# Shifted v rows of the first chunk by matmuls instead of a DRAM bounce, and the first 512 tokens in four passes of 128

## The chip, the cores and the metric

The kernel runs on one core of a Trainium2 chip. The metric is the device time of one execution in microseconds (us); lower is better. The kernel before has a median of 639.02 us over six runs (636.22 to 643.5). The profile that is read here is one execution of 640.18 us.

## The reference

A block of a transformer with 2048 tokens of width 576. A vector c gives six modulation vectors. The first half is attention with 32 heads of 18 elements in which each token looks at itself and at the tokens 2, 4, ... 14 places earlier (window W = 8, dilation 2). The second half is a gated product of width 4608 without an activation.

```python
mod = (silu(c) @ w_mod).reshape(1, 6, 1, 576)       # sa, ca, ga, sb, cb, gb
h = layernorm(x) * (1 + ca) + sa
q, k, v = split(h @ wqkv)                            # 32 heads of 18
idx = pos[:, None] - arange(8)[None, :] * 2          # masked where below 0
logits = einsum('bhsd,bhswd->bhsw', q, k[idx]) * 18 ** -0.5
o = einsum('bhsw,bhswd->bhsd', softmax(logits), v[idx])
x = x + ga * (o @ wo)
h = layernorm(x) * (1 + cb) + sb
x = x + gb * (((h @ w_gate) * (h @ w_up)) @ w_down)
```

## The kernel before

**Tiling.** The tokens are cut into chunks (`SIZES`: 128, 128, then seven of 256). The gate/up and down products work on 512 tokens (`CM`), which `DOWN` groups: the first 512 tokens take three passes over the gate and up weights (128, 128 and 256 tokens), each later 512 take one pass. After the last pass of a group follows the down product (`down`, L534). Weights of gate and up come in nine blocks of 512 columns. A ring of three buffers (`gm`, `gr`) streams them; the four blocks named in `KEPT` lie in the space of `wd`, the weights of down, until the first group's last pass is done with them. Then `block_done` loads that space with w_down, quarter by quarter (L271). `ORDER` is the order of the blocks in each pass.

**Attention of one chunk** has two generators. `project` does layernorm (L308 to L318), turns the rows into columns (`turn`, L325), applies sa and ca (L335, L337), and makes q, k (L360, evacuated by ACT at L362), the last 64 rows of both (L366 to L371) and v (L377). v is cast by ACT into `v_sb` with its elements in the order (d, h) (L380) and written to DRAM, `vd`, by ACT's DMA queue (L383). `attend` reads vd back through POOL's queue (L397): four shifted copies of each v row per load, two loads for 128 tokens, into `vsh` (three buffers). DVE multiplies q by shifted k (L410), PE sums over d (L419), PE transposes the logits (L427), DVE and ACT do the softmax (L437 to L445). Then DVE weights the v rows by attn (L450) and adds them in a tree (L451, L454, L455). The last addition writes `o_sb` in the order (h, d), one element in every 18th place. PE turns o_sb and multiplies by wo (L465); DVE applies ga, adds x and does the second layernorm; `h2T` is what gate and up read.

**Order of the work.** In the start, up to the first gate/up matmul, PE, DVE and ACT run in the order of the program (`manual_schedule`): `go` draws a generator forward to a named point. `warm` and the matmuls on zeros in `mod_columns` (L203) are filler for PE. `mod_columns` and `mod_row` (L219) make the modulation vectors. In the passes, `Pacer` hands out the pieces of the next chunks' attention between the matmuls of gate/up and down by the fractions in `AT`. Up to `AUTO` passes the engines' order is the scheduler's; after that PE's is the program's. Each engine executes in its own order, waits included. SP's queue loads the weights, ACT's queue writes vd, POOL's reads it and stores the output.

**PSUM.** `att` tiles have two buffers and serve all of attention; `ps_mlp` tiles have three and serve gate/up, down, mod_row and mod_columns.

## Time and profile before

| | |
|---|---|
| profiled execution | 640.18 us, its span 638.5 us |
| PE, DVE, ACT, POOL busy | 588.9, 343.8, 257.5, 49.2 us |
| first gate/up matmul | 54.1 us |
| first 512 tokens finished by PE | 252.2 us |
| vsh loads (L397) | 32 of 576 KB, median 5.4 us from issue to landing |
| vd writes (L383) | 16 of 144 KB, median 1.8 us |
| o_sb addition (L455) | 16, mean 2626 ns |
| vsh multiplication (L450) | 32, mean 1354 ns |

PE is the matmul, PEld its weight load, DVE, ACT and POOL the vector, scalar and general engines, SP the queue that issues most transfers; a small q after an engine marks what its queue issues. A row of the timeline has start, duration, engine, line, operation, and in brackets the idle time before it with what ended it. A row of a stretch has its bounds and length, then busy time of PE, PEld, DVE, ACT and POOL with the number of instructions, the granted TensorE clock as a share of full speed, the busy share of the DMA engines and their GB/s.

### The profile page before, as it was taken

To read this page: it belongs to the slowest core of one execution; us is meant where nothing else is said; L and a number is where in the kernel's file an instruction comes from. 1 tells how busy PE (TensorE), PEld (TensorE's weight loads), DVE (VectorE), ACT (ScalarE), POOL (GpSimd) and SP (SyncE) were. 2 spreads that over 40 slices of the span, in tenths; PEclk is the share of its full clock that TensorE was granted. 3 is DMA by queue.
4 is the path that set the end of the run, shared out by engine and by line. 5 is a ranking of instruction groups with operands and counts; after the bars stand their busy time and mean duration, and the time that the engine had idled before them with its cause. 6 is when DMAs were issued, how large, how long until landed. Compare 5 with 4: busy or idle time off the path is not lost.

```text
span 638.5 us, 11463 instructions
## 1 busy us (share of the span) xinstructions
PE 588.9 (92%) x4802; PEld 377.3 (59%) x4837; DVE 343.8 (54%) x654; ACT 257.5 (40%) x430; POOL 49.2 (8%) x97
## 2 busy tenths in 40 slices
PE   8759989779499989998999999989999999999996
PEld 4437868558377877454435786444446873333675
DVE  2455858857735786594548753683538732121111
ACT  2515565355336224444655223544552024444300
POOL 2101001100010111000000100001000000000000
PEclk9976989889889999999999999998999999999999
DMA  9999465407550042254510230434501003442000
GB/s 262 274 327 289 158 224 159 159 2 223 186 200 5 20 135 74 91 178 149 175 38 18 68 103 20 144 116 168 179 9 38 20 10 112 139 139 65 1 20 20
DMA packets 61133, 75.23 MB, mean 118 GB/s; under 512 B 4618, under 2 KB 54554, under 8 KB 61082
## 3 DMA queue, kind: packets, MB, share of 16 engines
q1 hardware_dynamic: 52970, 49.87, 25.9%
q0 software_dynamic: 5664, 22.12, 9.8%
q10 hardware_dynamic: 2448, 2.51, 1.1%
q8 instruction: 38, 0.62, 0.4%
q14 instruction: 13, 0.11, 0.0%
HBM read 69.75 MB, written 4.74 MB: 117 GB/s over the span
## 4 chain that ended last, share of the span: by engine, by line
PE 53%; DVE 11%; issue 8%; DMA 4%; ACT 1%; POOL 0%; SPq 0%; POOLq 0%; DVEq 0%; ACTq 0%
PE pgu L484 26%; PE acc L534 16%; PE pgu L491 4%; DMA vsh<-vd 3%; DVE vsh L450 3%; PE pv L377 2%; PE pw L465 2%; DVE vsh L451 1%; PE lgT L419 1%; DVE o_sb L455 1%; PE turnA L325 1%; ACT gu L521 1%; DVE hh L522 1%; PE pq L360 1%; DMA gr<-in_B_w_up_dram 1%
## 5 line engine op out<-in xcount | busy, mean ns | idle before, releaser
L484 PE MATMUL pgu<-h2T,gm 128*128 128x512 bf16 (+2 forms) x1313 | 241.9, 334 | 3.1 <-ACT gu L521 1.0
L521 ACT CAST gu<-pgu 128x1024 bf16<-128x1024 f32 (+1 forms) x162 | 140.6, 919 | 144.1 <-PE pgu L491 135.5
L484 PEld LDWEIGHTS <-gm 128*128 128x128 bf16 x1344 | 118.0, 100 | 109.4 <-issue 19.6
L534 PE MATMUL acc<-wd,hh 128*128 128x288 bf16 x1152 | 146.9, 286 | 0.0
L522 DVE TENSOR_TENSOR hh<-gu 128x512 bf16<-128x512 bf16 (+1 forms) x162 | 64.2, 401 | 133.7 <-ACT gu L521 133.7
L534 PEld LDWEIGHTS <-hh 128*128 128x128 bf16 x1152 | 111.9, 98 | 29.1 <-issue 1.7
L410 DVE TENSOR_TENSOR prod<-qT,kT 128x1280 bf16<-128x1280 bf16 (+1 forms) x72 | 46.3, 689 | 22.0 <-PE lgT L419 21.9
L450 DVE TENSOR_TENSOR vsh<-vsh,attn 128x2304 bf16<-128x2304 bf16 x32 | 42.5, 1354 | 14.5 <-DMA vsh<-vd 14.4
L397 POOL DMA_DIRECT2D vsh<-vd x32 | 24.2, 757 | 274.2 <-DMA vd<-v_sb 128.2
L360 PE MATMUL pq<-hT,wqk 128*128 128x256 bf16 (+1 forms) x360 | 42.9, 273 | 2.2 <-ACT hT L337 1.5
L377 PE MATMUL pv<-wv,hT 128*128 128x288 bf16 x160 | 25.0, 296 | 19.4 <-DVE kT L371 18.0
L455 DVE TENSOR_TENSOR o_sb<-vsh 128x576 bf16<-128x576 bf16 x16 | 42.0, 2626 | 0.3
L539 DVE TENSOR_TENSOR y<-acc,gb_bc 128x576 bf16<-128x576 f32 x16 | 12.3, 769 | 54.2 <-PE acc L534 54.2
L491 PE MATMUL pgu<-h2T,gr 64*128 64x512 bf16 (+2 forms) x336 | 40.1, 330 | 1.2 <-DMA gr<-in_B_w_up_dram 0.3
L360 PEld LDWEIGHTS <-wqk 128*128 128x128 bf16 x360 | 33.4, 105 | 10.5 <-issue 4.5
L484 PE MATMUL pgu<-h2T,wd 128*128 128x128 bf16 (+1 forms) x384 | 34.7, 244 | 0.2 <-DVE h2T L335 0.2
L377 PEld LDWEIGHTS <-hT 128*128 128x128 bf16 x160 | 15.1, 100 | 27.3 <-issue 22.3
L484 PEld LDWEIGHTS <-wd 128*128 128x128 bf16 x384 | 29.0, 101 | 3.8 <-issue 1.0
L317 ACT ACTIVATE xn<-x_t,ln_nmr,ln_rstd 128x576 bf16<-128x576 bf16 x32 | 27.6, 862 | 8.1 <-issue 4.2
L380 ACT CAST v_sb<-pv 128x288 bf16<-128x288 f32 x32 | 11.6, 405 | 39.0 <-PE pv L377 35.4
L308 DVE BATCH_NORM_STATS2 ln_stats<-x_t 128x6 f32<-128x288 bf16 x64 | 25.8, 440 | 0.4
L465 PE MATMUL pw<-wo,oT 128*128 128x288 bf16 x160 | 24.9, 306 | 1.0 <-DVE oT L458 0.9
(102 smaller groups left out, 397.4 us busy)
## 6 DMA issues: line engine op xcount, KB each, us to landing
vsh<-vd POOLq DMA_DIRECT2D x32, 576.0 KB, 5.4
gm<-in_B_w_gate_dram SPq DMA_DIRECT2D x27, 512.0 KB, 3.6
gm<-in_B_w_up_dram SPq DMA_DIRECT2D x27, 512.0 KB, 4.8
wd<-in_B_w_down_dram SPq DMA_DIRECT2D x4, 1152.0 KB, 5.8
wm<-in_w_mod_dram SPq DMA_DIRECT2D x4, 576.0 KB, 7.0
vd<-v_sb ACTq DMA_DIRECT2D x16, 144.0 KB, 1.8
out_dram<-y POOLq DMA_DIRECT2D x16, 144.0 KB, 2.0
wd<-in_B_w_gate_dram SPq DMA_DIRECT2D x4, 512.0 KB, 4.4
```

What stands on the lines that cost most here:

```text
L317: nc.scalar.activation(xn[:, j, 0:D], src[j][:], ACTF.Identity, bias=nmr[:, j:j + 1], scale=rstd[:, j:j + 1])
L360: nc.tensor.matmul(pq[:, gi, 0:C], lhsT=wqk[:, kt, w0:w0 + P], rhs=hT[:, kt, 0:C], start=(kt == 0), stop=(kt == KT - 1))
L377: nc.tensor.matmul(pv[q][:], lhsT=hT[:, kt, j * P:(j + 1) * P], rhs=wv[:, kt, q * 288:(q + 1) * 288], start=(kt == 0), stop=(kt == KT - 1))
L410: nc.vector.tensor_tensor(prod[:, 0:nm, 0:C], qT[:, 0:nm, 0:C], kT[:, 0:nm, off:off + C], ALU.mult)
L450: nc.vector.tensor_tensor(vsh[:], vsh[:], attn[:, j, ws, None, :].to_broadcast([P, WG, DH, H]), ALU.mult)
L455: nc.vector.tensor_tensor(o_sb[:, j, 0:D].rearrange("p (h d) -> p d h", d=DH), va[:, 0], va[:, 1], ALU.add)
L465: nc.tensor.matmul(pw[q][:], lhsT=oT[:, m, j * P:(j + 1) * P], rhs=wo[:, m, q * 288:(q + 1) * 288], start=(m == 0), stop=(m == KT - 1))
L484: nc.tensor.matmul(out(t), lhsT=gm[:, kt, t, i * P:(i + 1) * P], rhs=h2[:, kt, cs], start=(kt == 0 and (t == 0 or C > 256)), stop=False, s ...
L491: nc.tensor.matmul(outs[hf](t), lhsT=gr[rows, t, i * P:(i + 1) * P], rhs=h2[rows, KT - 1, cs], start=False, stop=True, skip_group_check=True)
L521: nc.scalar.copy(g, src)
L522: nc.vector.tensor_tensor(hh[:, fs, cs], g[:, :, 0, :], g[:, :, 1, :], ALU.mult)
L534: nc.tensor.matmul(acc[:, q, 0:288], lhsT=hh[:, f, j * P:(j + 1) * P], rhs=wd[:, f, q * 288:(q + 1) * 288], start=(f == 0), stop=(f == FT ...
```

## The change

For the first chunk of 128 tokens v is no longer read back from DRAM. A wider identity (`identw`) whose column window is moved by 2(7-w) is the stationary operand of two matmuls for each of the eight shifts; ACT copies each result into a `vsh` buffer. v is still written to vd, since chunk 1 reads it. DVE multiplies two shifts at a time by attn, and instead of DVE's additions 40 matmuls against the identity (five for each shift) add up in PSUM, which yields o in columns (`oTa`, `oTb`) without `turn`.

The order of o is (d, h) everywhere now: the last addition on DVE writes o_sb in place order, and wo is loaded with its rows in that order, by four transfers on ACT's queue, issued in the start after the first layernorm.

The first 512 tokens are four chunks and four passes of 128; `ORDER`, `AUTO`, `DOWN`, the pass in which the kept blocks are given up and the loads of x follow. There are 29 block loads into the ring instead of 27.

In the start, chunk 1's projection is drawn after the attention of chunk 0 is through, `mod_columns` for the second layernorm has no filler and stands before chunk 0's product with wo, and two warm matmuls are gone. DVE instead of ACT casts chunk 0's k. The short xn activations come after the long ones.

```diff
--- before.py
+++ after.py
@@ -31,17 +31,20 @@
 CH = 256
-SIZES = [128, 128, 256, 256, 256, 256, 256, 256, 256]
-DOWN = [[[0], [1], [2]], [[3, 4]], [[5, 6]], [[7, 8]]]
+SIZES = [128, 128, 128, 128, 256, 256, 256, 256, 256, 256]
+DOWN = [[[0], [1], [2], [3]], [[4, 5]], [[6, 7]], [[8, 9]]]
 FB = 4
-AUTO = 3
+AUTO = 4
 GU_BUFS = 3
 NB = FT // FB
-ORDER = [[0, 1, 2, 3, 4, 5, 6, 7, 8], [6, 7, 8, 5, 4, 3, 2, 1, 0], [2, 3, 4, 5, 8, 1, 0, 6, 7],
-         [0, 6, 7, 1, 2, 3, 4, 5, 8], [4, 5, 8, 0, 1, 2, 3, 6, 7], [3, 6, 7, 0, 1, 2, 4, 5, 8]]
+ORDER = [[0, 1, 2, 3, 4, 5, 6, 7, 8], [6, 7, 8, 5, 4, 3, 2, 1, 0], [8, 1, 0, 5, 4, 3, 2, 6, 7],
+         [2, 3, 4, 5, 0, 6, 7, 1, 8], [7, 1, 8, 0, 2, 3, 4, 5, 6], [4, 5, 6, 0, 1, 2, 3, 7, 8],
+         [3, 7, 8, 0, 1, 2, 4, 5, 6]]
 KEPT = [2, 3, 4, 5]
+KEPT_PASSES = 4
+LOAD_X = {3: 6, 4: 7, 6: 8, 7: 9}
 AT = dict(lg0=.06, lg1=.14, lgT=.19, hT=.24, q0=.29, q1=.34, k0=.39, k1=.44, qkr=.48, v0=.52, v1=.57,
-          oT=.66, wo0=.70, wo1=.74, h2T=.92)
+          ws=.64, oT=.66, wo0=.70, wo1=.74, h2T=.92)
@@ -90,10 +93,11 @@
-    ident = consts.tile([P, P], BF, name="ident")
-    nc.gpsimd.memset(ident[:], 0.0)
-    nc.gpsimd.affine_select(out=ident[:], in_=ident[:], compare_op=ALU.not_equal, fill=1.0, base=0,
-                            pattern=[[-1, P]], channel_multiplier=1)
+    identw = consts.tile([P, HALO + P], BF, name="identw")
+    nc.gpsimd.memset(identw[:], 0.0)
+    nc.gpsimd.affine_select(out=identw[:], in_=identw[:], compare_op=ALU.not_equal, fill=1.0, base=HALO,
+                            pattern=[[-1, HALO + P]], channel_multiplier=1)
+    ident = identw[:, HALO:HALO + P]
     ind = consts.tile([P, KT + 1, H], BF, name="ind")
@@ -176,7 +180,6 @@
     load_rows(nc.sync, wmC[:, :, D:2 * D], w_mod[:, 5 * D:6 * D])
-    load_rows(nc.sync, wo, A_wo)
     wmB = wm_tile()
@@ -184,9 +187,14 @@
+    def load_wo():
+        for dl in range(4):
+            n = len(range(dl, DH, 4))
+            nc.scalar.dma_start(wo[dl * H:(dl + 1) * H, 0:n, :], A_wo.rearrange("(h d) n -> h d n", d=DH)[:, dl::4, :])
+
     def silu_c():
         pc = att([P, KT], BF, "pc")
-        nc.tensor.transpose(pc[:], c_row[:], ident[0:KT, 0:KT])
+        nc.tensor.transpose(pc[:], c_row[:], identw[0:KT, HALO:HALO + KT])
         c_f = sp.tile([P, KT], F32, name="c_f")
@@ -196,11 +204,12 @@
-    def mod_columns(wm, vi):
-        pw = ps_mlp.tile([P, 2, 512], F32, name="warm", tag="mlp")
+    def mod_columns(wm, vi, fill):
+        pw = ps_mlp.tile([P, 2, 512], F32, name="warm", tag="mlp") if fill else None
         pm = ps_mlp.tile([P, 2, 512], F32, name="pm", tag="mlp")
         for kt in range(KT):
-            nc.tensor.matmul(pw[:, 0, :], lhsT=zeros[:, 0:P], rhs=zeros[:, 0:512], start=True, stop=True)
+            if fill:
+                nc.tensor.matmul(pw[:, 0, :], lhsT=zeros[:, 0:P], rhs=zeros[:, 0:512], start=True, stop=True)
             for bi in range(2):
@@ -249,7 +258,7 @@
         for b in order:
-            if b in KEPT and pi < 3:
+            if b in KEPT and pi < KEPT_PASSES:
                 continue
@@ -271,7 +280,7 @@
     def block_done(pi, b):
-        if pi == 2 and b in KEPT:
+        if pi == KEPT_PASSES - 1 and b in KEPT:
             k = KEPT.index(b)
@@ -315,6 +324,7 @@
             nc.scalar.activation(xn[:, j, 0:D], src[j][:], ACTF.Identity, bias=nmr[:, j:j + 1], scale=rstd[:, j:j + 1])
+        for j in range(ST):
             nc.scalar.activation(xn[:, j, D:], src[j][:, D - 64:], ACTF.Identity, bias=nmr[:, j:j + 1], scale=rstd[:, j:j + 1])
@@ -337,6 +347,8 @@
     scale = float(DH) ** -0.5
+
+    v_first = []
@@ -359,7 +371,8 @@
                                      start=(kt == 0), stop=(kt == KT - 1))
-            nc.scalar.copy(qT[:, m0:m0 + 2, 0:C] if t == 0 else kT[:, m0:m0 + 2, HALO:HALO + C], pq[:, :, 0:C])
+            (nc.vector.tensor_copy if ci == 0 and t == 1 else nc.scalar.copy)(
+                qT[:, m0:m0 + 2, 0:C] if t == 0 else kT[:, m0:m0 + 2, HALO:HALO + C], pq[:, :, 0:C])
         yield "qkr"
@@ -381,13 +394,23 @@
             nc.scalar.dma_start(vd[r0:r0 + P, :], v_sb[:])
+        if ci == 0:
+            v_first.extend(vshp.tile([P, WG, DH, H], BF, name="vsh") for _ in range(2))
+            for w in range(W - 1, -1, -1):
+                yield f"s{w}"
+                ps = ps_mlp.tile([P, 2, 512], F32, name="pvs", tag="mlp")
+                off = HALO - DIL * (W - 1 - w)
+                for q in range(2):
+                    nc.tensor.matmul(ps[:, q, 0:288], lhsT=identw[:, off:off + P], rhs=v_sb[:, q * 288:(q + 1) * 288],
+                                     start=True, stop=True)
+                nc.scalar.copy(v_first[w // WG][:, w % WG].rearrange("p (q d) h -> p q (d h)", q=2), ps[:, :, 0:288])
...
         x_t = x_tiles[ci]
-        if ci >= 2:
-            load_x(ci + 4, nc.gpsimd)
+        if ci in LOAD_X:
+            load_x(LOAD_X[ci], nc.gpsimd)
         vshs = {}
@@ -397,8 +420,9 @@
-        for u in ((0, 0), (0, 1), (1, 0))[0:ST + 1]:
-            load_vsh(*u)
+        if ci > 0:
+            for u in ((0, 0), (0, 1), (1, 0))[0:ST + 1]:
+                load_vsh(*u)
         lgs = small.tile([P, 2, CH], BF, name="lgs", bufs=1)
@@ -410,7 +434,7 @@
                 if i % 2 == 1:
-                    if i % WG == 1:
+                    if i % WG == 1 or ci == 0:
                         yield f"lg{g}"
@@ -443,18 +467,34 @@
         nc.vector.tensor_tensor(attn, dd, ssum[:, :, None, :].to_broadcast([P, ST, W, H]), ALU.mult)
-        for j in range(ST):
-            va, vb = vshs[j, 0], vshs[j, 1]
-            for hf, vsh in ((0, va), (1, vb)):
-                ws = slice(hf * WG, (hf + 1) * WG)
-                nc.vector.tensor_tensor(vsh[:], vsh[:], attn[:, j, ws, None, :].to_broadcast([P, WG, DH, H]), ALU.mult)
-            nc.vector.tensor_tensor(va[:], va[:], vb[:], ALU.add)
-            if j + 1 < ST:
-                load_vsh(j + 1, 1)
-            nc.vector.tensor_tensor(va[:, 0:2], va[:, 0:2], va[:, 2:4], ALU.add)
-            nc.vector.tensor_tensor(o_sb[:, j, 0:D].rearrange("p (h d) -> p d h", d=DH), va[:, 0], va[:, 1], ALU.add)
-        yield "oT"
-        banks = turn(o_sb, C)
+        if ci == 0:
+            banks = (att([P, 3, P], F32, "oTa"), att([P, 2, P], F32, "oTb"))
+            for w0 in range(W - 2, -1, -2):
+                vsh = v_first[w0 // WG]
+                ws = slice(w0 % WG, w0 % WG + 2)
+                nc.vector.tensor_tensor(vsh[:, ws], vsh[:, ws], attn[:, 0, w0:w0 + 2, None, :].to_broadcast([P, 2, DH, H]), ALU.mult)
+                yield "ws"
+                flat = vsh[:].rearrange("p w d h -> p (w d h)")
+                for w in (w0, w0 + 1):
+                    for m in range(KT):
+                        f0 = w % WG * D + m * P
+                        n = min(P, WG * D - f0)
+                        nc.tensor.matmul(banks[m // 3][0:n, m % 3, :], lhsT=flat[:, f0:f0 + n], rhs=ident,
+                                         start=(w == W - 2 and m in (0, 3)), stop=(w == 1), skip_group_check=True)
+            yield "oT"
+        else:
+            for j in range(ST):
+                va, vb = vshs[j, 0], vshs[j, 1]
+                for hf, vsh in ((0, va), (1, vb)):
+                    ws = slice(hf * WG, (hf + 1) * WG)
+                    nc.vector.tensor_tensor(vsh[:], vsh[:], attn[:, j, ws, None, :].to_broadcast([P, WG, DH, H]), ALU.mult)
+                nc.vector.tensor_tensor(va[:], va[:], vb[:], ALU.add)
+                if j + 1 < ST:
+                    load_vsh(j + 1, 1)
+                nc.vector.tensor_tensor(va[:, 0:2], va[:, 0:2], va[:, 2:4], ALU.add)
+                nc.vector.tensor_tensor(o_sb[:, j, 0:D].rearrange("p (d h) -> p d h", d=DH), va[:, 0], va[:, 1], ALU.add)
+            yield "oT"
+            banks = turn(o_sb, C)
         (nc.vector.tensor_copy if ci == 0 else nc.scalar.copy)(oT[:, 0:3, 0:C], banks[0][:, :, 0:C])
@@ -592,20 +632,33 @@
         warm(5)
         a0 = project(0)
         next(a0)
-        mod_columns(wmA, 0)
+        load_wo()
+        mod_columns(wmA, 0, True)
         go(a0, "q0")
         warm(3)
+        go(a0, "v0")
+        b0, a1 = attend_into_place(0), project(1)
+        next(b0)
+        go(a0, "s7")
+        next(b0)
+        next(a0)
+        next(b0)
+        next(a0)
+        next(b0)
+        next(a0)
+        go(a1, "hT")
+        next(b0)
+        next(a0)
+        go(b0, "ws")
         go(a0, None)
-        b0, a1 = attend_into_place(0), project(1)
-        go(b0, "lgT")
-        go(a1, "hT")
-        go(b0, "oT")
         mod_row(wmC, 0, ga_bc)
         mod_row(wmC, 1, gb_bc)
+        go(b0, "oT")
+        go(a1, "q0")
+        go(b0, "wo0")
+        mod_columns(wmB, 2, False)
+        go(b0, "h2T")
         go(a1, None)
-        warm(2)
-        go(b0, "h2T")
-        mod_columns(wmB, 2)
         setup_late()
         go(b0, None)
```

## The prediction

> **What bounds the kernel now.** First the page: PE is busy 92% of the span, and the missing tenths lie almost all before slice 16 (255 us). So the question is what PE waits for there. Second, the busy time by stage: the stretches are the start (to 54.1, the first gate/up matmul), the three passes over the first 512 tokens, and the down projection of those tokens.
> ```profile
> span 638.5 us, 11463 instructions
> ...
> PE   8759989779499989998999999989999999999996
> ...
> PEclk9976989889889999999999999998999999999999
> ```
> ```profile
> 54.10:88.10 34.00, 31.55 (x457) 26.74 (x457) 23.99 (x59) 20.06 (x44) 4.07 (x8) 0.95 0.74 238
> 88.10:136.90 48.80, 40.73 (x560) 33.84 (x561) 36.40 (x76) 24.93 (x54) 4.26 (x7) 0.92 0.36 118
> 136.90:201.30 64.40, 55.25 (x520) 43.16 (x520) 38.34 (x69) 29.58 (x47) 4.75 (x7) 0.90 0.48 153
> 201.30:252.20 50.90, 49.19 (x450) 39.24 (x448) 37.18 (x64) 15.60 (x33) 7.47 (x13) 1.00 0.21 71
> ```
> Columns: stretch, length, busy PE, PEld, DVE, ACT, POOL, granted clock, DMA share, GB/s. From 54.1 to 252.2 PE idles 198.1 - 176.7 = 21.4 us; the granted clock (0.95, 0.92, 0.90) takes up to 0.05 x 34 + 0.08 x 48.8 + 0.10 x 64.4 = 12 more, part of them while PE idles anyway. Third, PE in order of time: where the bounce of v through DRAM ends last.
> ```profile
> 36.95 0.38 PE L227 MATMUL warm<-zeros 128*128 128x512 bf16 x1
> 43.39 0.50 PE L325 MATMUL turnA<-ident,o_sb 128*128 128x128 bf16 x3 [6.06 <-DVE o_sb L455]
> 43.69 0.42 PE L325 MATMUL turnB<-ident,o_sb 128*128 128x128 bf16 x2
> 45.04 2.58 PE L465 MATMUL pw<-wo,oT 128*128 128x288 bf16 x10 [0.94 <-DVE oT L458]
> ```
> The bounce leaves 6 us visible; the rest of it (v written at 21.8, vsh in at 34.1 and 37.1) covers chunk 1's projection (29.8 to 36.9). Fourth, DVE around the worst stall, 8.39 us before pv at 175.06:
> ```profile
> 160.77 2.63 DVE L455 TENSOR_TENSOR o_sb<-vsh 128x576 bf16<-128x576 bf16 x1
> ...
> 167.82 1.36 DVE L450 TENSOR_TENSOR vsh<-vsh,attn 128x2304 bf16<-128x2304 bf16 x1 [3.84 <-DMA vsh<-vd]
> 169.21 1.36 DVE L451 TENSOR_TENSOR vsh<-vsh 128x2304 bf16<-128x2304 bf16 x1
> 170.60 0.76 DVE L454 TENSOR_TENSOR vsh<-vsh 128x1152 bf16<-128x1152 bf16 x1
> 171.39 2.62 DVE L455 TENSOR_TENSOR o_sb<-vsh 128x576 bf16<-128x576 bf16 x1
> 174.04 0.43 DVE L370 CAST kT<-pr 64x256 bf16<-64x256 f32 x1
> ```
> The kT cast, which frees pv's bank, stands behind a DMA and a 2.6 us strided write. Last, what the SP queue waits for (total, times, longest):
> ```profile
> SPq L245 <- DMA vd<-v_sb: 6.0, 2, 4.5
> ...
> SPq L143 <- DMA wqk<-in_A_wqkv_dram: 1.5, 1, 1.5
> ```
> An issuing queue halts, in order, until an earlier transfer lands: in the built program each of SP's and ACT's transfers waits for the one eight places earlier. That matters below.
>
> **Part 1, the start: 9.7 us longer (54.1 to 63.8).**
> (a) wo moves from SP to four transfers on ACT, ahead of ACT's two hT activations. In the built program the second waits for a wqk transfer and the fourth for the x tile of chunk 1. In this trace wqk landed at 13.1 and that x tile at 16.3 (SP's next issues start then); two wo quarters (0.37 MB at 269 GB/s: 1.4 us) now share the way, so ACT is free near 17.6 to 18.0. hT starts at 18.0, not 13.81: +4.2. If the x tile came early, this would be +0.
> (b) From the first hT activation to the second v_sb cast it is 7.9 us (13.81 to 21.73); PE has idled 3 us before, so I add 0.6 of the 3.4 us window at half clock: 26.5. The v write then waits, on ACT, for the last large w_mod load, which landed at 26.8 (issued 16.89, 9.9 us). ACT goes on at 27.2.
> (c) The shifted rows: 16 matmuls of 288 columns, 2 us on PE, but eight ACT copies of 576 columns. The rows for casts of 256 (372 ns) and 512 (587 ns) give 0.60 to 0.65 each. Order on ACT: three copies (to 29.0), Ln, Exp and xn of chunk 1 (its DVE statistics are done at 29.5; 0.4 + 0.2 + 0.87 + 0.43: to 31.4), lgs (31.8), then lg, three DVE steps, Exp, ssum, reciprocal, attn (0.3 + 1.45 + 0.4 + 1.4 with gaps: 35.6); four more copies end at 36.7, just after attn.
> (d) Two mod_row, 3.35 us at full clock at 24.56; they start when a PSUM buffer is free, 35.5, from a cold PE: 4.9, to 40.4. The four multiplications (0.76 each, as L454) hide under it. Forty identity matmuls at 60 ns: 42.8. Before, o_sb was ready at 43.33 and oT at 45.0: the whole bounce is worth 2 us once (a) and (b) are paid.
> (e) Then chunk 1's projection, which the bounce had covered, stands in the open. oT copy 0.5, turn 0.3, three hT on ACT 1.2, second turn 0.3, mod_columns 3.9 (five times 0.78), pw 2.6 at half clock: +8.8. From pw's end y, x, statistics, rstd and xn took 5.1 (47.4 to 52.5); with a second Ln/Exp pair ahead on ACT 5.4: +14.2. ACT's q and k casts stand behind xn, so the rest of the projection follows: 7.2 us (29.75 to 36.95) less two q groups already done plus turn and h2T: 6.8. First gate/up at 42.8 + 21.0 = 63.8. Before it was oT + 9.1.
> A rule of the Trainium skill weighed here: in "TensorE: Matmul & The Clock Gate", its part on the HAM clock gate, one busy window of about 3.4 us brings the full clock back. In this trace PE worked from 44.0 on, yet the clock stayed at 0.50 until 57.7, over mod_columns' one-column matmuls.
> ```profile
> 47.40:50.90 3.50, 3.47 (x40) 2.48 (x40) 3.41 (x12) 0.40 (x2) 0.00 (x0) 0.50 1.10 323
> ```
> The new mod_columns has no filler, so I take pw at its measured 2.58; by the rule it would be 1.4 and the start 1.2 shorter.
>
> **Part 2, the first 512 tokens: 7.8 us shorter (198.2 to 190.4).** Gate/up per block at 128 columns: 32 matmuls at 60 ns and 8 at 41: 2.2 us, 19.9 a pass; at 256: 32 at 109 and 8 at 68: 36.3. Two passes of 128 for one of 256 cost 3.5 more. "TensorE: Matmul & The Clock Gate", section on the back-to-back issue gap, speaks against the change: a stream of weight load and matmul at N=128 sustains about 81 ns. That would make 29 us a pass (360 x 81), some 18 us more for the two. But the row has it: 16 matmuls at 63.12, the next group at 64.11, 62 ns each.
> Pass 0 with 128 attended and 256 projected took 34.0. Projecting 128 instead saves 3.8 (pq 40 x 50 ns, half of pv 1.2, pr and turns 0.6); the kT wait comes sooner by 3.2 of PE's time while DVE's chain loses 2.2: +1.9 of stall; 0.9 of waiting for weights goes. Passes 0, 1, 2: 31.2, 29.7 (it begins warm), 32.5 (it projects 256 again, ends its waits for weights and DVE's chain is 2.2 shorter).
> Pass 3 plus down is before's pass 2 (115.3) less 16.4 of gate/up, with the same 512 tokens attended: 98.9. The 8.4 us stall stays: in this pass too four w_down loads refill the room of the kept weights, and the chunk's last vsh load and the weights of blocks 1 and 8 compete with them. PE comes to pv after 24 us, not 29.5; DVE has kT after 32, not 38. With the stall at 234 (1.69, behind an o_sb) down to 0.3 and 0.5 less at the first: 97.0.
> Three passes take 93.4 where two took 82.8, and the last with down 97.0 where it took 115.3: 190.4. What is won is before's pass 1, 8.1 us of it idle.
>
> **Part 3, afterwards: 5 us shorter.** wo's rows in d-major order let the last addition write o_sb unbroken: from 2.63 to about 0.45 (L471, also 576 columns, takes 0.454), 15 times. Most of it is hidden under PE. What shows: kT waits of 1.87 (292) and 3.16 (432) fall by 1.9 and 2.2, and the half-clock window after the second by about 1. Everything else there is PE at work: nothing.
> What leaves the queues: POOL loses two vsh issues of 0.75 us and 1.18 MB, and SP its 4.5 us wait for chunk 0's v write. SP then brings weights earlier, but nobody waits for them at 63.8: nothing. On the other side chunk 1's v is written only at 63.5, and DVE wants the rows 10 us into pass 0. Chunk 0's took 12 to 15 us from write to rows under a full DMA, the page's median is 1.8 + 5.4 plus issue. I take the second, so nothing; at worst +4.
> Weights: 29 blocks are loaded instead of 27, 2.4 MB; SP's queue has room (DMA is busy 0.21 to 0.48 of the time after 137), so they cost nothing; without that room, 4 us a block.
>
> **Sum.** +9.7 - 7.8 - 5.0 = -3.1 on the profiled 640.2 (span 638.5 and 1.7 around it): 637.1. The median of the runs, 639.0, is 1.2 under the profiled one: 636.
>
> **Rivals.** 0.5% (3.2 us) is about what this measurement tells from no change; the bounds are 635.8 and 642.2.
> - *The start shortens as it is written to* (20%): the transfers that ACT waits for land early. Without (a) and (b) the start is 58, and with the clock up during mod_columns 57: 629; with less stall in the short passes 624. For it: the trace shows when transfers landed in the old order of issue, not in the new one. Against: (e), which holds anyhow.
> - *The fourth pass starves* (25%), the other side: weights of blocks 1 and 8 (2.4 MB) stand behind 4.7 MB of w_down, with vsh beside them. At 270 GB/s that is 26 us, and PE needs block 8 26 us after the pass begins. I have this hidden by the kT stall; if it comes after it instead, each 0.27 MB late costs 1 us. From 6 us on the kernel is slower than before by a measurable step; 9 to 12 give 645 to 648. For it: SP took 16.4 us to issue the four loads (from 143.5).
> - *The short passes change nothing* (10%): their ends each wait for xn (before: 0.81, then 1.70 and 1.76), stalls move with the tokens and o_sb stays hidden: 640.
> My forecast has 45%, with its own range 631 to 642. The range of all, 627 to 647, reaches into both outer rivals. Faster: the first rival's 20, and 24 of the forecast's 45; same: 19 of it and 7 of the last; slower: 25, 2 and 3.
>
> **What would show it.** First pgu near 64 (58 or less: rival one). hT's ACT part at 18, the v write's issue after 26. o_sb additions near 0.45. The fourth pass begins near 157, and the 512 tokens end near 254. A wait of pv for kT of 6 to 9 us in the fourth pass; a wait of pgu for gm there would be rival two. No kT wait above 1.5 after 260. I am wrong if the start is not longer, or if the passes of 128 take over 33 us each.

## The result, and the profile after

| | before | after |
|---|---|---|
| median of the runs | 640.16 us (635.62 to 643.51, 20 runs) | 633.87 us (630.62 to 637.01, 10 runs) |
| ratio, 95% interval | | 0.9912 (0.988 to 0.9943) |
| profiled span | 638.5 us | 633.2 us |
| first gate/up matmul | 54.1 us | 63.91 us |
| first 512 tokens finished by PE | 252.25 us | 251.32 us |
| from there to the end | 386.25 us | 381.88 us |

The change makes the kernel 0.9% faster. The forecast was 636.0 us; the three parts were +9.7, -7.8 and -5.0, and they came out as +9.8, -10.7 and -4.4 (63.91 - 54.1; 187.41 - 198.15; 381.88 - 386.25). So the forecast looks right part by part. The experiments below show that two of the three parts do not mean what the forecast took them for.

The page of the changed kernel:

```profile
span 633.2 us, 12577 instructions
...
PE   6577999999969999999999999999999999999996
...
PEclk8876999999989999999999999999999999999999
```

The empty tenths are now in slices 0 to 3 (to 63 us), and one is left behind them, slice 11 (174 to 190 us). The rows by stretch (columns as in the table of before) give the same picture:

```profile
0.00:63.91 63.91, 43.33 (x393) 28.43 (x395) 22.43 (x69) 21.13 (x55) 5.81 (x23) 0.75 0.88 248
63.91:93.67 29.76, 28.79 (x483) 25.24 (x483) 19.54 (x56) 17.29 (x42) 5.26 (x10) 0.97 0.71 225
93.67:123.01 29.34, 28.14 (x483) 24.43 (x482) 20.43 (x61) 17.83 (x43) 2.23 (x5) 1.00 0.41 128
123.01:156.08 33.07, 31.89 (x497) 27.50 (x497) 22.18 (x61) 21.17 (x47) 2.99 (x6) 1.00 0.43 136
156.08:251.60 95.52, 87.53 (x968) 70.54 (x968) 64.03 (x134) 38.43 (x80) 11.96 (x20) 0.96 0.43 141
```

Three passes of 29.8, 29.3 and 33.1 us in which PE is busy all but 3.35 us: there the forecast had 31.2, 29.7 and 32.5. ACT's rows in the start show steps (a), (b) and (c):

```profile
12.73 4.26 ACTq L193 DMA_DIRECT2D wo<-in_A_wo_dram  x3
17.09 0.81 ACT L347 ACTIVATE hT<-turnB,modc 128x128 bf16<-128x128 bf16 x2 [7.75 <-DMA x_t<-in_A_x_dram]
...
28.03 0.35 ACTq L396 DMA_DIRECT2D vd<-v_sb  x1
28.42 1.72 ACT L406 CAST vsh<-pvs 128x576 bf16<-128x576 f32 x3 [3.14 <-DMA wm<-in_w_mod_dram]
```

The wo transfers hold hT until chunk 1's x tile is there, at 17.09, and the v write holds the copies until a w_mod load is there, at 28.4. And PE, with the two waits of the fourth pass:

```profile
48.70 2.58 PE L505 MATMUL pw<-wo,oT 128*128 128x288 bf16 x10
...
63.91 2.50 PE L524 MATMUL pgu<-h2T,gm 128*128 128x128 bf16 x26 [0.22 <-DVE h2T L345]
...
187.33 1.36 PE L390 MATMUL pv<-wv,hT 128*128 128x288 bf16 x5 [5.17 <-DVE kT L384]
...
235.35 1.26 PE L390 MATMUL pv<-wv,hT 128*128 128x288 bf16 x9 [1.44 <-DVE kT L384]
```

After 251.32 the two waits of pv for kT are 1.20 us each (290.75 and 428.71), where they were 1.87 and 3.16. The last addition of the attention has its new price (mean in ns after the comma):

```profile
L495 DVE TENSOR_TENSOR o_sb<-vsh 128x576 bf16<-128x576 bf16 x15 | 6.8, 454 | 0.3
```

### The profile page after: what moved, and what is told of

It reads as the page before. It is cut to its first block, busy times and chain, and to the rows that moved or that the text cites. A ratio compares the mean times of both kernels' runs of the same rounds, so it can differ in the third digit from the quotient of the medians.

```text
span 633.2 us, 12577 instructions
## 1 busy us (share of the span) xinstructions
PE 590.8 (93%) x5293; PEld 384.4 (61%) x5326; DVE 313.4 (49%) x698; ACT 265.7 (42%) x472; POOL 48.8 (8%) x100
## 4 chain that ended last, share of the span: by engine, by line
PE 51%; issue 5%; DMA 1%; DVE 1%; ACT 1%; SPq 0%; POOL 0%; POOLq 0%; DVEq 0%; ACTq 0%
PE pgu L524 27%; PE acc L574 13%; PE pgu L531 4%; PE pq L372 2%; PE pw L505 2%; DMA gm<-in_B_w_up_dram 1%; PE pv L390 1%; PE lgT L443 1%; PE turnA L335 1%; ACT gu L561 0%; PE turnB L335 0%; SPq L254 0%; POOL out_dram L582 0%; DVE ssum L466 0%; PE lg L451 0%
## 5 line engine op out<-in xcount | busy, mean ns | idle before, releaser
L524 PE MATMUL pgu<-h2T,gm 128*128 128x512 bf16 (+1 forms) x1473 | 240.4, 312 | 3.2 <-DVE h2T L345 1.3
L561 ACT CAST gu<-pgu 128x1024 bf16<-128x1024 f32 (+1 forms) x180 | 142.6, 844 | 140.3 <-PE pgu L531 135.4
L524 PEld LDWEIGHTS <-gm 128*128 128x128 bf16 x1504 | 120.1, 99 | 106.0 <-issue 17.6
L562 DVE TENSOR_TENSOR hh<-gu 128x512 bf16<-128x512 bf16 (+1 forms) x180 | 65.6, 368 | 136.3 <-ACT gu L561 136.2
L372 PE MATMUL pq<-hT,wqk 128*128 128x256 bf16 (+1 forms) x400 | 44.6, 265 | 8.9 <-ACT hT L347 4.6
L490 DVE TENSOR_TENSOR vsh<-vsh,attn 128x2304 bf16<-128x2304 bf16 x30 | 39.9, 1354 | 17.4 <-DMA vsh<-vd 17.3
L372 PEld LDWEIGHTS <-wqk 128*128 128x128 bf16 x400 | 34.8, 105 | 17.2 <-issue 11.3
L531 PE MATMUL pgu<-h2T,gr 64*128 64x512 bf16 (+1 forms) x376 | 40.9, 314 | 0.9
L579 DVE TENSOR_TENSOR y<-acc,gb_bc 128x576 bf16<-128x576 f32 x16 | 12.0, 752 | 50.8 <-PE acc L574 50.7
L524 PE MATMUL pgu<-h2T,wd 128*128 128x128 bf16 x512 | 34.4, 219 | 0.8 <-DVE h2T L345 0.5
L531 PEld LDWEIGHTS <-gr 64*128 64x128 bf16 x376 | 10.8, 95 | 25.1 <-issue 23.1
L321 ACT ACTIVATE ln_rstd<-ln_rstd 128x2 f32<-128x2 f32 (+1 forms) x20 | 3.7, 204 | 49.1 <-DVE ln_rstd L320 49.1
L582 POOL DMA_DIRECT2D out_dram<-y x16 | 8.8, 551 | 201.1 <-DVE y L581 201.1
```

The lines of the kernel that those rows point to most:

```text
L372: nc.tensor.matmul(pq[:, gi, 0:C], lhsT=wqk[:, kt, w0:w0 + P], rhs=hT[:, kt, 0:C], start=(kt == 0), stop=(kt == KT - 1))
L490: nc.vector.tensor_tensor(vsh[:], vsh[:], attn[:, j, ws, None, :].to_broadcast([P, WG, DH, H]), ALU.mult)
L524: nc.tensor.matmul(out(t), lhsT=gm[:, kt, t, i * P:(i + 1) * P], rhs=h2[:, kt, cs], start=(kt == 0 and (t == 0 or C > 256)), stop=False, s ...
L531: nc.tensor.matmul(outs[hf](t), lhsT=gr[rows, t, i * P:(i + 1) * P], rhs=h2[rows, KT - 1, cs], start=False, stop=True, skip_group_check=True)
L561: nc.scalar.copy(g, src)
L562: nc.vector.tensor_tensor(hh[:, fs, cs], g[:, :, 0, :], g[:, :, 1, :], ALU.mult)
```

## The experiments

The theory to be tested was that of the forecast: the start costs 9.8, the passes give back more, the order of o gives 4 to 5 besides. The rival was that the parts are not independent: what an earlier or later start is worth depends on what the first passes wait for. All ratios are against the kernel before, run beside them; "first 512" is the start of gate/up of the second group. The ratios are not plain quotients of the medians; the four columns before them are of one profiled execution each, which lay up to 1.9 us from the median of its kernel (3.6 in the last row but one), so 1 or 2 us between two rows of these columns are no difference that can be told.

| run | start | passes | first gate/up | third pass | first 512 | span | ratio (95%) |
|---|---|---|---|---|---|---|---|
| before | old | old | 54.1 | | 252.25 | 638.5 | 1 |
| order of o only | old | old | 51.97 | | 255.91 | 637.7 | 0.9956 (0.9927 to 0.9984) |
| passes only | old | new | 52.09 | 121.70 | 252.64 | 639.2 | 0.9982 (0.9951 to 1.0013) |
| order and passes | old | new | 50.66 | 121.31 | 249.70 | 632.4 | 0.9905 (0.987 to 0.9939) |
| after | new | new | 63.91 | 123.01 | 251.32 | 633.2 | 0.9912 (0.988 to 0.9943) |
| after, old passes | new | old | 64.12 | | 254.96 | 636.7 | 0.9925 (0.9891 to 0.996) |
| after, wo on SP | new | new | 55.57 | 123.46 | 252.19 | 634.1 | 0.9932 (0.9901 to 0.9963) |
| after, v on POOL | new | new | 61.87 | 120.59 | 248.62 | 630.5 | 0.9895 (0.9837 to 0.9953) |
| after, wo on SP, v on POOL | new | new | 56.95 | 122.47 | 249.82 | 631.7 | 0.9899 (0.9853 to 0.9945) |
| order and passes, v on POOL | old | new | 50.89 | 122.33 | 249.95 | 632.6 | 0.9921 (0.9889 to 0.9953) |
| after, filler | new | new | 65.67 | 124.22 | 252.44 | 634.3 | 0.9938 (0.9907 to 0.9969) |
| after, v on POOL, k on ACT | new | new | 61.77 | 119.99 | 246.57 | 627.9 | 0.9839 (0.98 to 0.9877) |
| the same, wo on SP | new | new | 58.16 | 124.83 | 251.47 | 632.8 | 0.983 (0.9791 to 0.9868) |
| the same, program order on PE | new | new | 57.61 | 123.89 | 250.10 | 631.1 | 0.9855 (0.9819 to 0.9892) |

The table already holds the main finding: with passes of 128 the first gate/up matmul lies anywhere between 50.7 and 65.7 us, and the third pass begins between 120.0 and 124.8 in all of them.

### The order of o alone

```diff
-    load_rows(nc.sync, wo, A_wo)
+    for dl in range(4):
+        n = len(range(dl, DH, 4))
+        nc.sync.dma_start(wo[dl * H:(dl + 1) * H, 0:n, :], A_wo.rearrange("(h d) n -> h d n", d=DH)[:, dl::4, :])
...
-                nc.vector.tensor_tensor(o_sb[:, j, 0:D].rearrange("p (h d) -> p d h", d=DH), ...
+                nc.vector.tensor_tensor(o_sb[:, j, 0:D].rearrange("p (d h) -> p d h", d=DH), ...
```

> The kernel before, with the order of o changed alone: the last addition writes o_sb unbroken, wo is loaded with its rows in (d, h) order by four transfers on SP in the old place. Theory (part 3 of the prediction, with more of it in the passes): the 16 additions fall from 2.63 to 0.45 us; the start stays at 54.1 within 1 us but for chunk 0's own addition (-2); the waits of pv for kT at 292 and 432 go, 381.6 to 382 us are left after the first 512 tokens where it was 386; two additions stand ahead of the kT cast in the pass with the 8.4 us wait, which falls to 4 to 6. Together 8 to 10 us faster, ratio 0.985 to 0.987. Rival: the additions are hidden under PE and the waits are set by the vsh loads; then less than 3 us.

Measured: 638.74 us, ratio 0.9956: the size that the rival gave, not the 8 to 10 us of the theory. After the first 512 tokens 381.79 us are left, as forecast, and the first gate/up comes 2.1 earlier. But the first 512 tokens take 203.94 us where they took 198.15, so that more than the start's gain is lost again. Part of it is in the table of waits of PE between 50 and 255 us (total, times, longest):

```profile
PE turnA L327 <- ACT xn L319: 5.9, 3, 2.4
PE pgu L486 <- DMA gm<-in_B_w_up_dram: 2.9, 1, 2.9
PE pgu L486 <- DMA gm<-in_B_w_gate_dram: 1.2, 1, 1.2
```

4.1 us of waiting for weights, where before had 0.9. So the order of o gives what part 3 says where the kernel is long, and a start that is 2 us shorter gives nothing.

### The passes alone

```diff
-SIZES = [128, 128, 256, ...]
-DOWN = [[[0], [1], [2]], [[3, 4]], ...]
-AUTO = 3
+SIZES = [128, 128, 128, 128, 256, ...]
+DOWN = [[[0], [1], [2], [3]], [[4, 5]], ...]
+AUTO = 4
+KEPT_PASSES = 4
```

with `ORDER` and the loads of x as in the change.

> The kernel before, with the first 512 tokens as four passes of 128 alone (old start, o_sb strided). Theory (part 2 of the prediction): first gate/up at 54.1; the first 512 tokens take 190 us where they took 198, less what the strided additions keep: -5 to -8, ratio 0.988 to 0.992. Rival A: the short passes win nothing, since their ends wait for xn and the stall only moves: -2 to +1. Rival B: from 54 on the first pass needs its nine blocks in 20 to 30 us, sooner than in the changed kernel, which began at 63.9; then waits of pgu for gm or gr of 3 us or more in the first pass.

Measured: 639.71 us, ratio 0.9982, which is no difference that can be told. The first 512 tokens take 200.55 us, not 190. Rival A, on this start: PE waits 2.4 us for kT at 72 and 2.3 for xn at 84 in the first pass; a wait for weights, rival B, has no row there, though SP stood 10.5 and 4.5 us behind v writes. What took 10.7 us off this stretch in the changed kernel is not the length of the passes by itself.

### Both on the old start

The edits of the two runs above together.

> Both other parts on the old start: the kernel before with four passes of 128 and the unbroken o_sb, wo by four transfers on SP, chunk 0 still through DRAM. It differs from the changed kernel only in the start. Theory: the new start costs its 9.8 us, so this is 633.9 - 9.8 - 1 = 621 to 626, ratio 0.970 to 0.978. Rival: the later start of the changed kernel hides the loading of weights; here the first pass starves for weights by 3 to 8 us and the ratio is 0.98 to 0.99.

Measured: 634.77 us, ratio 0.9905. The first gate/up comes 13.25 us earlier than in the changed kernel, and the first 512 tokens end 1.6 us earlier. The intervals of the two ratios are almost the same. So the new start, which is 13 us longer, costs next to nothing. That is the size that the rival gave. Of its mechanism, 3 to 8 us of waiting for weights, PE shows only 1.3 us here (none in the changed kernel). Between the runs with and without the order of o (this one and the passes alone) the end after the first 512 tokens falls from 386.56 to 382.70, part 3 once more. The first 512 tokens take 199.04 us here and 187.41 in the changed kernel. 8.0 of the 11.6 between them are idle time of PE (199.04 - 179.67 = 19.4 against 187.41 - 176.07 = 11.3), 3.6 are busy time at a lower clock (0.96 against 0.98, as many matmuls).

### The old passes on the new start

The changed kernel with the second run's constants taken back.

> The changed kernel with the first 512 tokens in three passes of 128, 128 and 256 as before: new start and unbroken o_sb, old passes. By the prediction (the passes give 7.8 wherever the start stands; by the trace 10.7): 641 to 645, ratio 1.002 to 1.008. By what the runs on the old start show (the passes alone give 1 us, with o_sb unbroken 4): 637 to 639, ratio 0.994 to 0.999. By the view that the time of the first passes is that of the weights and of chunk 1's attention, whenever the start ends: as with the order of o alone on the old start, 638.7, ratio 0.9956, with waits for weights in the first pass under 1 us where that run had 4.1.

Measured: 638.38 us, ratio 0.9925; the forecast's 1.002 to 1.008 is excluded. The first 512 tokens take 190.84 us with the old passes. So of the 10.7 us that this stretch lost in the changed kernel, 7.3 come with the late start and the order of o, and 3.4 with the passes of 128. This split is of one execution each; the ratios with and without the short passes, 0.9912 and 0.9925, do not differ. PE waited for no weights in the first passes here, where the order of o on the old start had 4.1 us.

### wo on SP: the late start made early

```diff
+    for dl in range(4):
+        n = len(range(dl, DH, 4))
+        nc.sync.dma_start(wo[dl * H:(dl + 1) * H, 0:n, :], A_wo.rearrange("(h d) n -> h d n", d=DH)[:, dl::4, :])
     wmB = wm_tile()
...
         next(a0)
-        load_wo()
```

> The changed kernel with one edit: the four wo transfers on SP, ahead of the last large w_mod load, not on ACT ahead of hT. By the order of transfers in the built program the v write then waits for an early transfer (wv) and no longer for the last large w_mod load, so (a) and (b) both go. Theory (prediction, first rival): hT's ACT part at 13.8 and not 17.1, the v write issued at 21 to 22 and not 28.0, first gate/up at 57 to 59 and not 63.9; 627 to 629 us, ratio 0.981 to 0.984. Rival: ACT's eight copies and the softmax chain set the end of the start (c to e); then first gate/up at 61 or later, and the time within 3 us of the changed kernel's 633.9.

Measured: hT's part on ACT at 11.46, the v write issued at 19.62, the first gate/up at 55.57: 8.3 us earlier. (a) and (b) are real. The time is 637.27 us, ratio 0.9932: not faster than the changed kernel. PE at the end of the first pass, and what SP's queue stood behind:

```profile
82.50 0.62 PE L527 MATMUL pgu<-h2T,gm 128*128 128x128 bf16 x8 [1.71 <-DMA gm<-in_B_w_gate_dram]
84.59 0.34 PE L338 MATMUL turnA<-identw,xn 128*128 128x128 bf16 x3 [1.48 <-ACT xn L329]
89.99 1.36 PE L527 MATMUL pgu<-h2T,gm 128*128 128x128 bf16 x11 [2.30 <-DMA gm<-in_B_w_gate_dram]
```
```profile
SPq L143 <- DMA vd<-v_sb: 13.1, 1, 13.1
SPq L257 <- DMA vd<-v_sb: 4.7, 1, 4.7
```

SP issued nothing from about 44 to 57 us: its next transfer came, in order, after chunk 1's v write, which ACT could issue only at 55.09. Between 50 and 60 us the DMA engines were busy 0.23 of the time. In the changed kernel SP stands 10.1 us behind the same write (55.0 to 65.1), but there the passes begin only at 63.9.

### The v writes of chunks 0 and 1 on POOL's queue

```diff
-            nc.scalar.dma_start(vd[r0:r0 + P, :], v_sb[:])
+            (nc.gpsimd if ci < 2 else nc.scalar).dma_start(vd[r0:r0 + P, :], v_sb[:])
```

In the built program POOL's transfers stand in a row of their own, and SP no longer comes after these two writes. This edit was made in three kernels. In the changed kernel:

> The changed kernel with one edit: the v rows of chunks 0 and 1 are written to DRAM by POOL's queue, not by ACT's, so neither ACT nor SP waits in order around them ((b) goes, (a) stays). Theory now: SP's 10.1 us wait for chunk 1's v write (53 to 63) goes, DMA keeps on in that stretch; ACT's 3 us wait for w_mod goes, first gate/up at 60.5 to 61.5 and not 63.9; no wait for weights in the first pass, so the gain stays: 630 to 632 us, ratio 0.984 to 0.988. Rival (weights are loaded at the rate of the DMA engines, SP's wait costs nothing): the first two passes get longer by what the start gains, 633 to 635.

With wo on SP as well:

> The changed kernel with wo on SP and the v rows of chunks 0 and 1 written by POOL's queue: (a) and (b) go, and SP's wait for a v write (13.1 us with wo on SP alone, with DMA busy 0.23 from 50 to 60) goes with them. Theory now (the earlier start was given back because SP stood behind the v write while the weights of the first passes were due): first gate/up at 55.5 as with wo on SP alone, waits of pgu for gm under 1 us in the first 40 us after it, the third pass begins at 115 to 117 and not 123.5; 624 to 628 us, ratio 0.974 to 0.980. Rival (bandwidth: 17 MB must pass before the first pass can end, whoever issues them): the third pass begins at 121 to 123.5 again and the time stays at 634 to 637.

On the old start with new passes and order:

> The old start with four passes of 128 and the unbroken o_sb (the run on the old start), with the v rows of chunks 0 and 1 written by POOL's queue. Theory now: SP's waits of 14.1 and 4.9 us for v writes go, so the first pass has its weights: first gate/up at 50 to 52, third pass at 110 to 114 and not 121.3, 622 to 627 us, ratio 0.970 to 0.979. Rival (bandwidth): third pass at 119 to 121, 632 to 635. Second rival: POOL's issue delays the rows of chunk 0 by 1 to 3 us, and the first gate/up comes at 52 to 54.

Measured: 633.6, 635.3 and 635.87 us, ratios 0.9895, 0.9899 and 0.9921, which do not differ by the timing. In the second and third the gain that the theory gave did not come: the third pass begins at 122.47 and 122.33, not at 115 to 117 and 110 to 114. The traces tell more. In the first kernel the start gains 2.04 us (61.87), all of it and a little more is still there at the end of the first 512 tokens (248.62, 2.7 earlier), and the span is 2.7 shorter. In the second the first gate/up is 7 us earlier, of which 1.5 are left at 249.82. In the third nothing is won. The rows of SP's waits for a v write explain the difference. The first kernel has none. The second, and the third:

```profile
SPq L255 <- DMA vd<-v_sb: 18.6, 1, 18.6
```
```profile
SPq L248 <- DMA vd<-v_sb: 14.3, 1, 14.3
```

Only two writes were moved. With the passes begun early, SP now reaches the transfer that comes after chunk 2's v write long before that write is issued (76.83 in the second kernel, 71.9 in the third), and stands there. The stretches from 60 to 90 of the second kernel, the last two columns are the DMA share and GB/s:

```profile
60.00:70.00 10.00, 9.97 (x190) 8.83 (x189) 6.71 (x19) 6.04 (x14) 4.16 (x9) 1.00 0.84 283
70.00:80.00 10.00, 7.71 (x120) 6.59 (x118) 7.19 (x16) 5.20 (x13) 0.00 (x0) 1.00 0.07 22
80.00:90.00 10.00, 6.90 (x96) 5.52 (x93) 4.96 (x19) 3.94 (x11) 1.50 (x2) 0.89 0.85 268
```

The DMA engines stand all but idle for 10 us in the middle of the first pass, while one of its nine blocks and half of another are still to be loaded. So bandwidth, the rival of all three expectations, is not what makes these weights late in this kernel; the in-order queue is.

PE in this kernel shows no wait for weights, though, but one of 2.86 us for xn, which ends at 86.62. When the last block of the first pass landed can be read from its issue and its time to landing (the last number of the second row, in us). In the second kernel, and in the changed kernel, where the gate half of this block was issued at 75.30:

```profile
82.30 0.53 SPq L255 DMA_DIRECT2D gm<-in_B_w_gate_dram  x1
gm<-in_B_w_gate_dram SPq DMA_DIRECT2D x1, 512.0 KB, 7.4
90.11 2.01 PE L527 MATMUL pgu<-h2T,gm 128*128 128x128 bf16 x24
```
```profile
gm<-in_B_w_gate_dram SPq DMA_DIRECT2D x1, 512.0 KB, 7.2
90.27 2.09 PE L524 MATMUL pgu<-h2T,gm 128*128 128x128 bf16 x32
```

With the early start the block lands at 89.7 and PE begins it 0.4 us later; with the late one it lands at 82.5 and lies ready for 7.8 us. So the wait for xn seems to hide one for weights. In the four runs with the new start made early, PE begins this block within 1 us of its landing; in the late ones with passes of 128 (begun at 62 to 66) it lies ready for 7.8 to 10.8 us. On the old start with passes of 128 it is 3.1 to 4.0 us, so there the last block is not what holds PE.

The clock has a part as well. The first two passes as one stretch, in the first kernel and in the second:

```profile
61.87:120.59 58.72, 56.45 (x965) 48.94 (x964) 39.95 (x116) 35.11 (x84) 8.33 (x17) 1.00 0.52 161
56.95:122.47 65.52, 58.84 (x965) 50.48 (x965) 40.34 (x116) 35.36 (x84) 8.09 (x17) 0.97 0.51 162
```

As many matmuls take 6.8 us longer: 4.4 are idle time of PE (6.68 against 2.27), 2.4 are busy time, at a granted clock of 0.97 and not 1.00.

### PE in the order of the program

```diff
-AUTO = 4
+AUTO = 0
```

with wo on SP, the two v writes on POOL's queue, and the k casts of the next section.

> As the run with wo on SP, v rows on POOL's queue and all k casts on ACT, but PE takes the order of the program in the first four passes too, where it was the scheduler's. If the loss of the first pass is the scheduler's order (work of the pass standing behind a wait for xn on PE): that wait falls from 2.9 to under 1 and the time is 2 to 4 us under the same run with the scheduler's order. If it is chunk 1's attention: the third pass begins within 1 us of it. If the scheduler's order fitted the late transfers: the first 512 tokens take 3 us longer or more.

Measured: 632.73 us, ratio 0.9855, no faster than the same kernel with the scheduler's order (0.983, next section). The third pass begins at 123.89, 0.9 before that of the same kernel, which by the number is the second case. The trace shows something else: the wait for xn is gone, and in its place stand the weights:

```profile
87.18 0.40 PE L527 MATMUL pgu<-h2T,gm 128*128 128x128 bf16 x4 [3.39 <-DMA gm<-in_B_w_gate_dram]
89.99 3.17 PE L527 MATMUL pgu<-h2T,gm 128*128 128x128 bf16 x28 [2.41 <-DMA gm<-in_B_w_up_dram]
```
```profile
80.72 0.53 SPq L255 DMA_DIRECT2D gm<-in_B_w_gate_dram  x1
```
```profile
82.50 0.66 SPq L255 DMA_DIRECT2D gm<-in_B_w_up_dram  x1
```

The two halves of the last block are issued at 80.72 and 82.50, after SP stood 16.4 us behind chunk 2's v write (from 63), and PE waits for each. The scheduler's order had put other work and the turn of xn ahead of that block. That the wait for xn in that order was free, because the block behind it was not there either, follows from this pair of traces and from the time at which the block landed; it was not measured by itself.

### The k casts on ACT

```diff
-        copy = nc.scalar.copy if ci == 1 else nc.vector.tensor_copy
+        copy = nc.vector.tensor_copy if ci == 0 else nc.scalar.copy
```

with the v writes of chunks 0 and 1 on POOL's queue, first alone and then with wo on SP too.

> The changed kernel with the v rows of chunks 0 and 1 written by POOL's queue (as in the run before, profiled at 630.5) and one further edit: ACT casts the last 64 rows of k in every chunk but the first, not in chunk 1 alone. Theory: the waits of pv for kT (5.1 us at 184.8, 1.6 at 232.7) are DVE's order, the cast stands behind a multiplication that waits for rows; on ACT they go, and with them the half-clock time after the first: 4 to 7 us, 624 to 627 profiled, ratio 0.978 to 0.984. Rival: the same rows are late for o_sb, so the wait moves to the turn of o_sb or to pw, or ACT's evacuation of gate/up comes late; less than 2 us gained.

> As the run above, with wo on SP too, so that the first gate/up comes 5 us sooner (56 to 57.5). With v rows on POOL's queue and wo on SP the first pass had no wait for weights but took 6 us longer, with waits of 1.8 for kT and 2.9 for xn. If kT's cast is what holds it: the third pass begins at 117 to 119 and the time is 3 to 4 us under the run above, 620 to 623. If the attention of chunk 1 holds it (its rows, the products and the layernorm, some 30 us from its v write): the wait for xn grows by what kT's wait loses, third pass at 120.5 to 122.5, and the time is within 2 us of the run above.

Measured: 631.31 us, ratio 0.9839, and 630.9 us, ratio 0.983. These are the fastest two, and they beat both the kernel before and the changed kernel; against v on POOL alone (0.9895) the intervals overlap. The earlier start again adds nothing to speak of (the second kernel's profiled execution, 634.46 us, is its longest, so its row of the table stands too high). Of the second expectation the time fits the second case (within 2 us of the run above), its trace neither: the wait of 1.8 for kT in the first pass is gone, but that for xn is 2.86 as before, and the third pass begins at 124.83. Against the same kernel with k on DVE the span falls from 630.5 to 627.9, less than expected. The wait at 233 is gone. The larger one has only changed its name: PE, ACT and DVE in the first of the two kernels,

```profile
184.04 1.29 PE L390 MATMUL pv<-wv,hT 128*128 128x288 bf16 x7 [4.75 <-ACT kT L384]
```
```profile
182.01 0.58 ACT L561 CAST gu<-pgu 128x512 bf16<-128x512 f32 x1 [4.12 <-DVE hh L562]
...
183.62 0.37 ACT L384 CAST kT<-pr 64x256 bf16<-64x256 f32 x1
```
```profile
180.36 1.36 DVE L490 TENSOR_TENSOR vsh<-vsh,attn 128x2304 bf16<-128x2304 bf16 x1 [5.11 <-DMA vsh<-vd]
181.63 0.28 DVE L562 TENSOR_TENSOR hh<-gu 128x256 bf16<-128x256 bf16 x1
```

DVE stands behind the rows of v; the product hh (L562) stands behind DVE, the evacuation of gate/up (two `gu` buffers) behind hh, and ACT's k casts behind that. This is the rival of the first expectation. What costs the 5 us is the vsh load: POOL issues it only at 172.84, when DVE's addition (171.19 to 172.54) has freed its buffer, and it lands 7.5 us later, where the median is 5.3 in this run, with the DMA engines busy 1.02 of the time between 170 and 180. Issuing it sooner, with one more buffer, was not tried.

### Filler in the second mod_columns

```diff
-        mod_columns(wmB, 2, False)
+        mod_columns(wmB, 2, True)
```

> The changed kernel with the filler back in the second mod_columns (one matmul of 512 zero columns for each of its five steps). By the Trainium skill's rule on the clock gate (TensorE: Matmul & The Clock Gate, the part on the HAM clock gate) the clock comes back over the busy filler: pw takes 1.3 to 1.6 us and not 2.58, mod_columns grows by 1 to 2, first gate/up within 1 us of 63.9. By the prediction (the clock stays at 0.50 over one-column matmuls in spite of filler, as it did before): pw 2.58, first gate/up 1 to 2 us later. In either case the time is within 2 us of the changed kernel's 633.9.

Measured: 636.04 us, ratio 0.9938; first gate/up 65.67, 1.8 later. PE, and the two halves of the stretch in which the granted clock is 0.50 (45.9 to 52.7; after it the clock is full again):

```profile
48.14 0.61 PE L212 MATMUL warm<-zeros 128*128 128x512 bf16 x1
48.55 0.79 PE L217 MATMUL pm<-sc,wm 128*128 128x1 bf16 x12
49.81 0.74 PE L217 MATMUL pm<-sc,wm 64*128 64x1 bf16 x12 [0.47 <-DMA wd<-in_B_w_up_dram]
50.47 2.48 PE L505 MATMUL pw<-wo,oT 128*128 128x288 bf16 x10
```
```profile
45.90:49.30 3.40, 3.40 (x41) 2.40 (x40) 0.00 (x0) 0.45 (x2) 0.00 (x0) 0.50 0.97 299
49.30:52.70 3.40, 2.93 (x24) 2.11 (x24) 0.23 (x2) 0.00 (x0) 0.00 (x0) 0.50 0.83 250
```

PE is busy for the whole of the first half, the clock stays at 0.50 for the second, and pw still takes 2.48, against 2.58 without. In the changed kernel, without filler, it is the same: PE is busy 3.40 of 3.40 us from 45.3 on, and the clock is at half until 52.2. So here, as in the trace of before, the step that used the measured 2.58 holds, and the rule of the Trainium skill ("TensorE: Matmul & The Clock Gate", the part on the HAM clock gate), that a busy window brings the clock back, is not borne out over such matmuls. The time is 2.2 us above the changed kernel's, a little more than expected, and by the ratios (0.9938 and 0.9912) no difference that can be told.

## Why the prediction was right, and where it was not

**The time.** 636.0 was forecast, 633.87 measured, and the range held it. Each part's size is close, too. What was wrong is the sum as a sum, and that it still came near is in part luck: the prices of parts 1 and 2, of which neither holds by itself, almost cancel (+9.7 and -7.8 forecast, +9.8 and -10.7 measured), and part 3 is left.

**Part 1, the start.** As a duration it is exact: 63.91 for 63.8. (a) hT came at 17.09 and not at 18.0, for the transfer that the forecast named; (b) the copies began at 28.4, not 27.2, for the load that it named; (c) the copies took 0.57 each and ended at 36.75; (d) the identity matmuls ended at 43.0; (e) from there to the first gate/up 20.9, with mod_columns 3.5 instead of 3.9. Moving wo showed that (a) and (b) hold up the start by 8.3 us. As a cost it is wrong. The same kernel with the old start, 13 us shorter, is not faster beyond the interval, and moving wo away, 8.3 us of start, gains nothing.

**Part 2, the first 512 tokens.** -10.7 instead of -7.8; the lengths of the four passes are right to 1.8 us. The row of 62 ns a matmul holds, not the 81 that the prediction weighed from the Trainium skill ("TensorE: Matmul & The Clock Gate", the back-to-back issue gap). In the first pass of the changed kernel 32 take 1.95 us, 61 ns each:

```profile
81.92 1.95 PE L524 MATMUL pgu<-h2T,wd 128*128 128x128 bf16 x32
```

But the step "What is won is before's pass 1, 8.1 us of it idle" is refuted: on the old start the short passes give nothing that can be told, and on the new start 3.4 us of the stretch in one pair of executions and nothing that can be told in the time. Two of its sums do not come out, both by less than 1 us: 3.2 sooner less 2.2 is 1.0 of stall, not 1.9, and nine blocks of 32 matmuls at 60 ns and 8 at 41 are 20.2 us, not 19.9.

**The step that failed** is "SP then brings weights earlier, but nobody waits for them at 63.8: nothing", and the sum that adds +9.7 and -7.8 as if each stood alone. Nobody waits at 63.8 because the start is late. Begun at 50 to 58, the first pass comes to its last blocks about when they land or before, since SP stood in order behind a v write that comes only as PE and ACT get to it. So the start's length and the passes' idle time are one quantity: a longer start is paid back, in part by the weights that arrive during it. That the weights have a part in this is shown by the waits for them (4.1, 4.0 and 5.8 us in three runs with an early start, 1.3 or less in the other five, none in the late ones) and by the landing of the last block, which in the runs with the new start made early comes within 1 us before PE begins it. That SP's wait makes them late is shown by the idle DMA engines beside it. How much of the 13 us is theirs and how much that of chunk 1's attention, whose xn waits in the same pass, is not separated. A kernel with every v write off SP's row, which would separate it, was not run.

**Part 3.** -4.4 for -5.0, in every kernel with the unbroken order (381.0 to 382.7 left after the first 512 tokens, 386.3 to 386.6 without). This is the part of the gain that stands by itself. The waits at 292 and 432 fell less than forecast, by 0.7 and 2.0 to 1.20 each; with the smaller gaps PE's idle time is 2.6 us shorter there (386.25 - 373.11 against 381.88 - 371.37), and the other 1.7 are busy time of PE, 373.11 against 371.37, at a clock of 1.00 and not 0.99.

**The stall in the fourth pass.** 5.17 us, forecast 6 to 9, and 1.44 for 0.3 at 235. That it is kT's was right; that the cast's place on DVE is its cause was only half of it: with the k casts on ACT 4.75 us of the wait stayed, because they stood behind the same load of v rows, while the wait at 235 went.

**The rivals.** The first (a shorter start, 629 or 624) did not come by itself, and it was wrong in its price: when moving wo shortened the start to 55.57, the time was 637. The second (the fourth pass starves) did not come: no wait for gm there. The third (short passes change nothing) is what happens on the old start.

## What to carry to other kernels

Before a longer or shorter start is booked as cost or gain, ask what the first loop behind it waits for: if it is weights that stream in the background, the start is partly hidden in that stream, and its length and the loop's idle time must be priced together. Look at every queue that runs in order for a small, late write between large, early loads; here a 144 KB write held up the weights by up to 18.6 us at a time, and starts made earlier by up to 13 us gained nothing that could be told. And when a wait is named after the last engine in a chain, move that engine's work only after following the chain to its first link, here a DMA.

## What the runs showed of the hardware

- The last addition of 576 bf16 columns takes 2.63 us when it writes one element in every 18th place, and 0.454 us when it writes them in a row.
- Matmuls of 128 columns with a new weight tile each ran at 61 ns for 32 in a row (1.95 us) in the first passes.
- Over one-column matmuls PE was busy for 3.40 of 3.40 us at a granted clock of 0.50, and the clock stayed at 0.50 for 3.4 us more, with a filler matmul of 512 columns for every twelve (45.9 to 52.7) and without (45.3 to 52.2).
